# GpSimd's powers of two: multiply and add zero, where it multiplied alone

## The chip, the cores and the metric

The kernel runs on one core of one Trainium2 chip. The metric is the device time of one execution in microseconds (us). A core has TensorE (PE, with PEld for its weight loads), VectorE (DVE), ScalarE (ACT), GpSimd (POOL) and SyncE (SP), which each work through a queue of their own and wait for one another by semaphores.

## The reference

From one input x (1 x 2048 x 512, bf16) two branches are computed and mixed by a gate. Branch a is attention with 32 heads of 16; branch b mixes neighbouring rows and ends in an MLP of width 1792.

```
g = sigmoid((x * gate_w).sum(-1))
a:  q, k, v = x @ wqkv              # 32 heads of 16
    p = softmax(q k^T * 16 ** -0.5)
    a = (p v) @ wo
b:  h  = gelu(layernorm(x) @ w1);   quarters of h shifted by +1, -1, +2, -2 rows
    x1 = x + shifted(h) @ w2
    b  = x1 + gelu(layernorm(x1) @ w3) @ w4
out = g * a + (1 - g) * b
```

## The kernel before

**Units.** The rows are 4 chunks of 512 queries. A unit is one chunk and four heads: 32 units. In a unit the scores of one head against 128 keys are a block of 128 x 512 (keys by queries), 64 blocks a unit. TensorE writes blocks into PSUM (`score`, line 749); the exponentials turn them into bf16 weights; TensorE multiplies those with v and a column of ones into an accumulator (`attend_block`, line 924), so that the sum of the weights comes along; `finish_unit` divides.

**Slots.** Blocks go through slots. A slot has three blocks for ScalarE, which takes their exponential in one instruction (`expo`, line 912, 128 x 1536). The scores carry a factor of 65536/ln 2, which the exponential's scale takes out again. From slot 34 on a slot can hold two blocks for ScalarE (128 x 1024) and a third, in the PSUM tile `dsc`, whose exponential VectorE and GpSimd work out without ScalarE. `wants_whole` chooses these; there are 254 of them, taken in 127 pairs.

**An exponential without ScalarE** (`whole`). The score is 65536 times the exponent of two.

- `dump` (VectorE, line 845) adds a bias, clamps and converts to int32 in a tile `y`, of which there are two buffers, shared with the output's `dd` (line 535). The high 16 bits of an element are the whole part of the exponent, the low 16 the fraction.
- `factor` (GpSimd, line 852) reads the low halves and makes a linear factor in f16, in the tile `once`, by a multiply and an add.
- `two` (GpSimd, line 858) reads the high halves, multiplies by 128 and writes 16-bit integers, whose bits are a bf16 power of two, in the tile `power`. Behind it the y buffer is free.
- When both blocks of a pair are there, VectorE makes three products over 128 x 1024: `square` (line 866, from `once` alone), `linear` (line 870, `power` times `once`) and `cubic` (line 883). `power`, `cube` and `once` are the three terms that TensorE sums in the accumulator in place of one exponential (`attend`).

There are three sets of (`power`, `once`, `cube`); two have these names, the third is cut out of a tile named `more`. At most two pairs are under way (`CHAINS`), and a new dump is planned only if a y buffer is free by the plan (`YBUFS` = 2).

**Order.** The instruction order on every engine is fixed when the kernel is built: a planner keeps a clock for each engine, and always issues what can start first by its own list of costs. For both GpSimd steps this cost is `POOLT` = 0.62 us, whatever their form; the clocks also keep VectorE's instructions that share the port with GpSimd apart from GpSimd's. On the chip the engines then follow that order and wait where the plan was off. Between the attention blocks the planner puts the work of branch b (projections at line 217, `gelu_pair` at lines 357 to 390, layer norms with the transposed copies at line 347), and `fill` (line 1103) puts matmuls with a zero weight where TensorE would be idle.

Of the kernel before, what the change touches and what calls it, by code (L numbers as in the profile page):

```python
# [11 lines left out]
ALU = mybir.AluOpType  # L12
# [6 lines left out]
U16 = mybir.dt.uint16  # L19
# [12 lines left out]
def kernel(  # L32
# [13 lines left out]
    nc = tc.nc  # L46
# [101 lines left out]
    for j in range(4):  # L148
        src = A_wo.rearrange("(G j a d) n -> j a d G n", j=4, a=2, d=DH)[j]
        for a in range(2):  # L150
            nc.sync.dma_start(
                out=wo_pad[32 * j + 1:32 * j + 1 + DH, :, :].rearrange("d (G a) n -> a d G n", a=2)[a],
# [39 lines left out]
    def post(engine, rank, cost, fn, ready=0.0, shared=False):  # L192

        state["n"] += 1
        queue[engine].append((rank, state["n"], cost, fn, ready, shared or engine == "pool"))
# [626 lines left out]
    def whole(k, dsc, n, kt, j, ready):  # L822

        if whole_pair["open"] is None:
            whole_pair["chains"] += 1
            whole_pair["open"] = (n, j)
            whole_pair["tiles"] = (room.popleft(), [])
            r = 0  # L830
        else:
            whole_pair["open"] = None
            r = 1
            heads = {j, whole_pair["tiles"][1][0][1]}

            whole_pair["heads"] = () if whole_pair["heads"] and whole_pair["heads"][0] == n else (n, heads)
        whole_pair["last"] = k
        whole_pair["y"] += 1
        (power, once, cube), pair = whole_pair["tiles"]
        pair.append((kt, j))  # L840
        times = {}

        def dump(end):
            y = ypool.tile([P, CH], I32, tag="y", name="y")
            nc.vector.tensor_scalar(out=y[:], in0=dsc[:], scalar1=(127.0 + SHIFT) * 65536.0, scalar2=65536.0,  # L845
                                    op0=ALU.add, op1=ALU.max)
            dumped[k] = end
            halves = y[:].bitcast(U16).rearrange("p (n k) -> p n k", k=2)
            lo, hi = halves[:, :, 0], halves[:, :, 1]

            def factor(end):
                nc.gpsimd.tensor_scalar(out=once[:, r, :].bitcast(F16), in0=lo, scalar1=UK * LN2 / 65536.0, scalar2=UK * (UX - LN2 / 2),  # L852
                                        op0=ALU.mult, op1=ALU.add)
                if r == 1:
                    post("vector", 2, 0.68, square, end, True)

            def two(end):
                nc.gpsimd.tensor_scalar(out=power[:, r, :].bitcast(U16), in0=hi, scalar1=128.0, scalar2=None, op0=ALU.mult)  # L858
                times["power"] = end
                whole_pair["y"] -= 1  # L860

            post("pool", 1, POOLT, factor, end + 0.05)
            post("pool", 1, POOLT, two, end + 0.05)

        def square(end):
            nc.vector.tensor_tensor(out=cube[:].bitcast(F16), in0=once[:].bitcast(F16), in1=once[:].bitcast(F16), op=ALU.mult)  # L866
            post("vector", 2, 0.68, linear, lambda: max(end, times["power"]) if "power" in times else None, True)

        def linear(end):
            nc.vector.tensor_tensor(out=once[:], in0=power[:], in1=once[:].bitcast(F16), op=ALU.mult)  # L870
            both = state["credit"] > TWO and not state["done"]
            if both:
                post("vector", 2, 0.41, more, end, True)
            else:
                post("vector", 2, 0.68, cubic, end, True)

        def more(end):
            nc.vector.tensor_scalar(out=cube[:].bitcast(F16), in0=cube[:].bitcast(F16), scalar1=1.0, scalar2=None, op0=ALU.add)
            post("vector", 2, 0.68, lambda end: cubic(end, 2), end, True)

        def cubic(end, count=3):

            nc.vector.tensor_tensor(out=cube[:], in0=once[:], in1=cube[:].bitcast(F16), op=ALU.mult)  # L883
            whole_pair["chains"] -= 1
            products.append((n, pair, (power, cube) if count == 2 else (power, cube, once), end, (power, once, cube)))

        post("vector", 0, 0.69, dump, ready)
# [317 lines left out]
```

## Time and profile before

| | before |
|---|---|
| median of three runs | 920.33 us (919.62 to 920.62) |
| profiled execution | 923.89 us |
| its span | 920.9 us |
| mean granted clock of TensorE | 0.973 |
| GpSimd: line 852, multiply and add | 174 + 80 instructions, 736 and 730 ns in the mean |
| GpSimd: line 858, multiply | 174 + 80 instructions, 1530 and 1555 ns in the mean |

The profile is of one execution. The span runs from its first to its last instruction; the difference to the execution's own time lies around it. A line such as `L858 POOL TENSOR_SCALAR power<-y 128x512 uint16<-128x512 uint16 x174 | 266.2, 1530 | 0.0` is a group of instructions: source line, engine, operation, output and input with shape and type, count, busy us in all, mean ns of one, and the idle time of that engine just before them with what ended it. Idle time of an engine that others do not wait for costs nothing. A group under a name from the program, `power` or `more`, may be the same line with another buffer.

### The profile page before, as it was taken

To read this page: it belongs to the slowest core of one execution; us is meant where nothing else is said; L and a number is where in the kernel's file an instruction comes from. 1 tells how busy PE (TensorE), PEld (TensorE's weight loads), DVE (VectorE), ACT (ScalarE), POOL (GpSimd) and SP (SyncE) were. 2 spreads that over 40 slices of the span, in tenths; PEclk is the share of its full clock that TensorE was granted. 3 is DMA by queue.
4 is the path that set the end of the run, shared out by engine and by line. 5 is a ranking of instruction groups with operands and counts; after the bars stand their busy time and mean duration, and the time that the engine had idled before them with its cause. 6 is when DMAs were issued, how large, how long until landed. Compare 5 with 4: busy or idle time off the path is not lost.

```text
span 920.9 us, 15816 instructions
## 1 busy us (share of the span) xinstructions
PE 822.1 (89%) x5977; PEld 246.2 (27%) x5977; DVE 782.2 (85%) x1213; ACT 862.1 (94%) x735; POOL 580.4 (63%) x552
## 2 busy tenths in 40 slices
PE   8998988989898998998988899998899898899886
PEld 3222322222222222222222222222222222222221
DVE  5648699899999999888999887899876989998865
ACT  6899999999999999999999899999899999999984
POOL 3117576567686556887654887586566747698850
PEclk9999799999999999999999799999899999999988
DMA  9300100000002000001000000100000000000000
GB/s 232 100 14 13 59 2 12 13 13 14 9 7 92 13 13 13 13 4 34 13 13 13 1 13 14 36 13 13 2 12 14 13 31 1 18 13 14 14 13 23
DMA packets 30772, 22.22 MB, mean 24 GB/s; under 512 B 17256, under 2 KB 26216, under 8 KB 30696
## 3 DMA queue, kind: packets, MB, share of 16 engines
q1 hardware_dynamic: 29064, 20.04, 7.4%
q10 hardware_dynamic: 1632, 1.18, 0.5%
q8 instruction: 46, 0.75, 0.4%
q14 instruction: 30, 0.25, 0.1%
HBM read 17.04 MB, written 2.35 MB: 21 GB/s over the span
## 4 chain that ended last, share of the span: by engine, by line
DVE 38%; POOL 23%; PE 15%; issue 12%; ACT 9%; DMA 1%; POOLq 0%; DVEq 0%; ACTq 0%; SPq 0%
POOL power L858 9%; ACT pt L912 9%; POOL once L852 8%; DVE y L845 7%; PE stage L749 4%; PE acc L924 4%; DVE cube L866 4%; DVE once L870 4%; POOL more L858 4%; DVE cube L883 3%; POOL more L852 3%; DVE yh L390 2%; DVE more L866 2%; PE ps_y L217 2%; PE ps L217 2%
## 5 line engine op out<-in xcount | busy, mean ns | idle before, releaser
L912 ACT ACTIVATE pt<-stage 128x1536 bf16<-128x1536 f32 (+1 forms) x694 | 830.9, 1307 | 41.3 <-PE stage L749 17.8
L749 PE MATMUL stage<-qT,kT 32*128 32x512 bf16 x1794 | 277.6, 391 | 45.0 <-ACT pt L912 26.0
L852 POOL TENSOR_SCALAR once<-y 128x512 f16<-128x512 uint16 x174 | 128.0, 736 | 220.3 <-DVE y L845 213.6
L858 POOL TENSOR_SCALAR power<-y 128x512 uint16<-128x512 uint16 x174 | 266.2, 1530 | 0.0
L845 DVE TENSOR_SCALAR y<-dsc 128x512 int32<-128x512 f32 x254 | 173.1, 683 | 54.2 <-PE dsc L749 23.9
L924 PE MATMUL acc<-pt,vp 128*17 128x512 bf16 (+1 forms) x1794 | 188.8, 393 | 8.7 <-DVE accsb L987 8.5
L749 PEld LDWEIGHTS <-kT 32*128 32x128 bf16 x2048 | 78.4, 91 | 297.8 <-issue 227.5
L858 POOL TENSOR_SCALAR more<-y 128x512 uint16<-128x512 uint16 x80 | 124.4, 1555 | 0.0
L924 PEld LDWEIGHTS <-vp 128*17 128x17 bf16 (+1 forms) x2302 | 67.2, 89 | 142.7 <-issue 124.3
L749 PE MATMUL dsc<-qT,kT 32*128 32x512 bf16 x254 | 98.5, 388 | 0.3 <-DVE y L845 0.3
L852 POOL TENSOR_SCALAR more<-y 128x512 f16<-128x512 uint16 x80 | 58.4, 730 | 59.4 <-DVE y L845 48.3
L217 PE MATMUL ps_y<-xnT,w 128*128 128x512 bf16 x288 | 84.6, 382 | 11.8 <-DVE yh L390 9.9
L866 DVE TENSOR_TENSOR cube<-once 128x1024 f16<-128x1024 f16 x87 | 79.2, 910 | 13.0 <-POOL once L852 12.7
L1103 PE MATMUL acc<-wq,zero 128*128 128x512 bf16 x254 | 89.4, 395 | 0.0
L870 DVE TENSOR_TENSOR once<-power,once 128x1024 bf16<-128x1024 bf16 x87 | 68.2, 784 | 1.6 <-POOL power L858 1.5
L217 PE MATMUL ps<-w,g2T 128*128 128x512 bf16 x224 | 67.9, 390 | 1.4 <-DVE x_sb L462 0.9
L883 DVE TENSOR_TENSOR cube<-once,cube 128x1024 bf16<-128x1024 bf16 x87 | 64.9, 745 | 1.1
L390 DVE TENSOR_SCALAR yh<-ps_y 128x512 bf16<-128x512 f32 x72 | 49.0, 681 | 2.2 <-PE ps_y L217 2.1
L866 DVE TENSOR_TENSOR more<-more 128x1024 f16<-128x1024 f16 x40 | 37.1, 927 | 5.6 <-POOL more L852 5.6
L370 ACT ACTIVATE sq<-sq 128x1024 bf16<-128x1024 bf16 x36 | 39.6, 1106 | 0.0
L924 PE MATMUL acc<-cube,vp 128*17 128x512 bf16 x174 | 33.3, 402 | 3.2 <-DVE cube L883 3.0
L217 PEld LDWEIGHTS <-w 128*128 128x128 bf16 x288 | 23.1, 97 | 45.7 <-issue 36.0
(101 smaller groups left out, 743.9 us busy)
## 6 DMA issues: line engine op xcount, KB each, us to landing
bcs<-rec_d SPq DMA_DIRECT2D x31, 256.0 KB
w<-in_B_w_dram SPq DMA_DIRECT2D x2, 1792.0 KB
x_sb<-in_A_x_dram SPq DMA_DIRECT2D x14, 128.0 KB
out_dram<-ot SPq DMA_DIRECT2D x14, 128.0 KB
w<-in_B_w_dram SPq DMA_DIRECT2D x2, 512.0 KB
wkv<-in_A_wqkv_dram ACTq DMA_DIRECT2D x1, 512.0 KB
wo_pad<-in_A_wo_dram SPq DMA_DIRECT2D x8, 64.0 KB
den<-accsb SPq DMA_DIRECT2D x31, 8.0 KB
```

The costliest lines, as they stand in the source:

```text
L217: nc.tensor.matmul(*args, **kwargs)
L390: nc.vector.tensor_scalar(out=yh[:, r, :], in0=ps[:], scalar1=0.5, scalar2=None, op0=ALU.mult)
L749: nc.tensor.matmul(out, lhsT=kT[G][32 * j:32 * j + 32, cc, o:o + P], rhs=qTs[(c, G)][32 * j:32 * j + 32, a, :], start=True, stop=True, til ...
L845: nc.vector.tensor_scalar(out=y[:], in0=dsc[:], scalar1=(127.0 + SHIFT) * 65536.0, scalar2=65536.0, op0=ALU.add, op1=ALU.max)
L852: nc.gpsimd.tensor_scalar(out=once[:, r, :].bitcast(F16), in0=lo, scalar1=UK * LN2 / 65536.0, scalar2=UK * (UX - LN2 / 2), op0=ALU.mult, o ...
L858: nc.gpsimd.tensor_scalar(out=power[:, r, :].bitcast(U16), in0=hi, scalar1=128.0, scalar2=None, op0=ALU.mult)
L866: nc.vector.tensor_tensor(out=cube[:].bitcast(F16), in0=once[:].bitcast(F16), in1=once[:].bitcast(F16), op=ALU.mult)
L870: nc.vector.tensor_tensor(out=once[:], in0=power[:], in1=once[:].bitcast(F16), op=ALU.mult)
L883: nc.vector.tensor_tensor(out=cube[:], in0=once[:], in1=cube[:].bitcast(F16), op=ALU.mult)
L912: nc.scalar.activation(out=pt[:, 0:w], in_=stages.pop(k)[:, 0:w], func=ACT.Exp, scale=LN2 / 65536.0)
L924: nc.tensor.matmul(accs[n][32 * j:32 * j + M, :], lhsT=lhsT, rhs=p, start=(kt == 0), stop=(kt == NT - 1), skip_group_check=True, tile_posi ...
L1103: nc.tensor.matmul(acc[:], lhsT=zero[:], rhs=wq[:, 0, :], start=False, stop=False, skip_group_check=True)
```

## The change

In `two`, the instruction on GpSimd gets a second step: after the multiplication by 128 it adds 0.0. Its input, its output and its place in the queue stay, and so do the planner's costs. All else is as before.

```diff
             def two(end):
-                nc.gpsimd.tensor_scalar(out=power[:, r, :].bitcast(U16), in0=hi, scalar1=128.0, scalar2=None, op0=ALU.mult)
+                nc.gpsimd.tensor_scalar(out=power[:, r, :].bitcast(U16), in0=hi, scalar1=128.0, scalar2=0.0, op0=ALU.mult, op1=ALU.add)
                 times["power"] = end
                 whole_pair["y"] -= 1
```

## The prediction

> **What bounds the kernel now.** I read the first part of the page (busy time by engine), then the chain that ended last, then the costliest groups, and then went to the waits of single lines. "power" and "more" are both names of the tile that the changed line 858 writes; "more" is the third set of buffers.
>
> ```profile
> PE 822.1 (89%) x5977; PEld 246.2 (27%) x5977; DVE 782.2 (85%) x1213; ACT 862.1 (94%) x735; POOL 580.4 (63%) x552
> ...
> DVE 38%; POOL 23%; PE 15%; issue 12%; ACT 9%; DMA 1%; POOLq 0%; DVEq 0%; ACTq 0%; SPq 0%
> POOL power L858 9%; ACT pt L912 9%; POOL once L852 8%; DVE y L845 7%; PE stage L749 4%; PE acc L924 4%; DVE cube L866 4%; DVE once L870 4%; POOL more L858 4%; DVE cube L883 3%; POOL more L852 3%; DVE yh L390 2%; DVE more L866 2%; PE ps_y L217 2%; PE ps L217 2%
> ...
> L852 POOL TENSOR_SCALAR once<-y 128x512 f16<-128x512 uint16 x174 | 128.0, 736 | 220.3 <-DVE y L845 213.6
> L858 POOL TENSOR_SCALAR power<-y 128x512 uint16<-128x512 uint16 x174 | 266.2, 1530 | 0.0
> L845 DVE TENSOR_SCALAR y<-dsc 128x512 int32<-128x512 f32 x254 | 173.1, 683 | 54.2 <-PE dsc L749 23.9
> ...
> L858 POOL TENSOR_SCALAR more<-y 128x512 uint16<-128x512 uint16 x80 | 124.4, 1555 | 0.0
> ...
> L390 DVE TENSOR_SCALAR yh<-ps_y 128x512 bf16<-128x512 f32 x72 | 49.0, 681 | 2.2 <-PE ps_y L217 2.1
> ```
>
> ScalarE, 94% busy with the exponentials, is the floor. GpSimd is busy only 63%, yet it holds 23% of the chain, and line 858 alone 13% (9 and 4), about 120 us. Both facts go together if GpSimd's work comes in bursts: idle in total, late inside a burst. So the question is not how much GpSimd time is saved but how much idle time of ScalarE goes back to GpSimd. ScalarE's idle time is seen by stretches of the span:
>
> ```profile
> 0.00:23.00 23.00, 20.15 (x107) 7.54 (x107) 12.73 (x30) 15.77 (x19) 8.93 (x30) 1.00 0.95 232
> 23.00:46.00 23.00, 22.12 (x123) 6.45 (x122) 15.98 (x38) 18.55 (x20) 3.22 (x3) 1.00 0.36 100
> ...
> 897.00:920.00 23.00, 14.79 (x90) 4.35 (x87) 13.29 (x17) 11.72 (x9) 0.00 (x0) 0.89 0.07 23
> sum 920.00, PE 822.06 PEld 246.25 DVE 782.15 ACT 862.07 POOL 580.37; mean PE 20.55 PEld 6.16 DVE 19.55 ACT 21.55 POOL 14.51
> ```
>
> The columns are PE, PEld, DVE, ACT, POOL busy, the granted clock, the DMA share and GB/s. Without the first two stretches and the last, ScalarE is busy 862.07 - 15.77 - 18.55 - 11.72 = 816.0 of 851 us: 35 us of idle time in the middle. That is the most that any change to this pipeline can give.
>
> **The change part by part.** One operand pair changes in one instruction, which is issued 254 times (174 + 80). Nothing is moved, no wait is added, the planner's cost for it (0.62) stays, so every queue keeps its order. The output is the same number. What can change is the duration of line 858.
>
> ```profile
> L858 POOL TENSOR_SCALAR power<-y x174: 1479/1485/2449, 66.2 to 890.7; 128x512 uint16<-128x512 uint16 x174
> ...
>   DVE y L845: 24.2, 43
>   DVE dd L535: 7.5, 8
>   DVE once L870: 1.5, 4
>   DVE more L870: 0.9, 3
> ```
>
> ```profile
> L852 POOL TENSOR_SCALAR once<-y x174: 610/618/1643, 65.7 to 890.1; 128x512 f16<-128x512 uint16 x174
> ```
>
> (Minimum, median and maximum in ns, the first and last start, and for line 858 who waited for it: us and times.) Line 852 is the nearest row there is: the same engine, the same tile y (its other 16-bit halves, same stride), the same 512 elements a partition, but multiply and add; median 618 ns. Line 858 multiplies alone and takes 1485 ns. So the form with more arithmetic takes 867 ns less. Two differences remain between them: the missing second step, and the output type (uint16 against f16). If the missing step is the cause, the changed line takes 618; if the type is, it stays at 1485. For the type, the nearest rows are on VectorE: line 845 converts f32 to int32 at 683 ns, line 390 f32 to bf16 at 681 ns, so there an integer output costs nothing. It is another engine, hence only a leaning. I take 618 ns, with 1485 as the other end for a change without effect; an end above 1485 is priced among the rivals.
>
> The Trainium skill has a rule that speaks against this change: "GPSIMD Engine Reference", section 3.1 on side-by-side cycle accounting, says that an elementwise body of at most two operations is bound by the port at about 1.03 cycles an element. By it one step and two cost the same, 512 elements some 440 ns, and the change would do nothing. Line 852 fits it (618 ns with what an instruction costs besides); line 858 at 1485 ns doesn't, so this trace shows that something in line 858's form falls outside it.
>
> GpSimd's busy time would drop by 254 x 0.867 = 220 us, to 360. Nearly all of that lies beside other work. What reaches the end is seen in one burst, in order of time:
>
> ```profile
> 168.52 1.49 POOL L858 TENSOR_SCALAR power<-y 128x512 uint16<-128x512 uint16 x1
> ...
> 170.04 0.69 DVE L845 TENSOR_SCALAR y<-dsc 128x512 int32<-128x512 f32 x1 [1.00 <-POOL power L858]
> ...
> 170.65 0.41 DVE L347 COPY xnT<-ps_t 128x512 bf16<-128x512 bf16 x1
> ...
> 171.12 1.02 PE L217 MATMUL ps_y<-xnT,w 128*128 128x512 bf16 x4 [0.99 <-DVE xnT L347]
> ...
> 172.56 1.02 ACT L912 ACTIVATE pt<-stage 128x1024 bf16<-128x1024 f32 x1 [0.58 <-PE dsc L749]
> ```
>
> There are two y buffers, and line 858 reads a buffer last. The third dump of a burst (line 845) waits 1.00 us for it; behind the dump in VectorE's queue stands the copy of xnT, for which TensorE waits 0.99; behind that stand the next scores, for which ScalarE waits 0.58. At 618 ns line 858 would have ended at 169.14, before the dump was due, and the three waits go. GpSimd's pace in the burst falls from 0.62 + 1.49 = 2.1 us a dump to 1.24, near the one exponential of 1.02 that passes with each dump.
>
> How much of it there is in all: line 858 held VectorE up 58 times for 34.1 us (24.2 + 7.5 + 1.5 + 0.9), 0.59 us each, less than the 0.867 saved, so nearly all of these waits go. The squares wait too, for the first step of GpSimd queued behind line 858:
>
> ```profile
> DVE cube L866 <- POOL once L852: 12.7, 21, 1.2
> ...
> DVE more L866 <- POOL more L852: 5.6, 11, 1.0
> ```
>
> All VectorE waits for GpSimd in the timeline come to 55 us (95 waits). To see what arrives at ScalarE I went through its gaps in the timeline between 64 and 897 us: 71 gaps of 0.15 us or more, 31.1 us. In 31 of them, 13.9 us, VectorE waited for GpSimd within the 4 us before (at 5 us it would be 16.8). The first and the last of the 31:
>
> ```profile
> 85.19 10.49 ACT L912 ACTIVATE pt<-stage 128x1536 bf16<-128x1536 f32 x9 [0.70 <-PE stage L749]
> ...
> 883.53 2.79 ACT L912 ACTIVATE pt<-stage 128x1536 bf16<-128x1536 f32 x2 [0.47 <-PE stage L749]
> ```
>
> So 55 us of VectorE waits become about 14 us of ScalarE gaps, a quarter; the rest is slack. I take 13 us: nearly all of the 13.9, a little kept back because a few squares will still wait for line 852. What is late next is TensorE: the remaining 17 us of gaps stay, in which VectorE itself waited for TensorE's scores. The sum: the profiled execution took 923.89 us (its span 920.9), so 923.89 - 13 = 910.9; it lies 3.6 us above the median of the runs, 920.33, against which the forecast is 907.3, in round terms 907. Its own range: half of the attributed gaps, 7 us (913.5), to three quarters of all 31 us, 23 us (897), since a pipeline that stays near its plan may also lose gaps that I couldn't trace.
>
> **The rivals.** *No effect*: the type of the output, not the missing step, costs the time, or the single step was never slow for the reason I think. Line 858 stays at about 1485 ns, GpSimd at 580 us, the time at 920.3. For it: no row shows a uint16 output on GpSimd with two steps. Against: the 683 and 681 ns on VectorE. The rule of the page named above would give this time too, though it would have the present line fast already.
>
> *A wait takes its place*: line 858 gets fast, but VectorE loses as much where the two meet.
>
> ```profile
> L866 DVE TENSOR_TENSOR cube<-once x87: 623/1059/1092, 68.4 to 890.8; 128x1024 f16<-128x1024 f16 x87
> ```
>
> The square mostly starts together with line 858 and then takes 1059 ns where the fastest took 623. If GpSimd's earlier starts cost the second and third product of each of the 127 pairs (87 + 40) 0.4 us too, VectorE has up to 127 x 0.8 = 102 us more work; a quarter of it would reach ScalarE, 25 us; half of that cancels the gain: 920. Against: GpSimd starts as many instructions as before, and each would be over sooner.
>
> *Slower*: the slow path is the type's, and there the added step costs on top. It is priced by the nearest rows of GpSimd:
>
> ```profile
> L478 POOL MEMSET hT<- 128x8 bf16 x1 | 0.1, 100 | 0.0
> ```
>
> An instruction with next to no data takes 100 ns. Two steps in line 852 cost 618 - 100 = 518, one 260; in line 858 one step costs at most 1485 - 100 = 1385. With 260 more, the 58 waits grow by 15 us and a burst gets longer; by a quarter to a half, 4 to 8 us: 924 to 928. With 1385 more, line 858 takes 2870 ns and the pair with 736 beside it 3.6 us; the dumps come on average each (890.7 - 66.2) / 253 = 3.26 us, so GpSimd would set the pace from about 2500 ns on, and 254 x 3.6 = 914 us between the start at 66 and a tail of 29 gives 1009. I name 928 as its time, the near row being the one of the same engine and the same arithmetic.
>
> **How the numbers follow.** Line 858 near 618 ns with the waits gone: 0.66, 897 to 913.5, at 907. No effect: 0.18, at 920.3. The place taken: 0.05, at 920. Slower: 0.11, at 924 and more. I give the first so much since two rows that differ in so little differ by 867 ns in the direction of the change, and no more than that since one of their two differences isn't touched. A run of this kernel repeats within about 0.1%, and a change of 0.2% (1.8 us) is about what can be told from none. So faster 0.66, same 0.23, slower 0.11. The range runs from 896 to 922: it takes in the forecast's own range and the two cases of no change, and leaves out the slower case and a twentieth below, together under two tenths.
>
> **What would show it.** Right: line 858's median near 618 ns; GpSimd near 360 us; VectorE's waits for line 858 from 34 us to under 5; ScalarE's middle idle time from 35 to about 22 us; line 858 gone from the top of the chain. Line 858 still at 1485 puts the type in the step's place and the time at 920. Line 858 at 618 with ScalarE's idle time unchanged makes my attribution of gaps wrong: the gaps would then be TensorE's own, with the GpSimd waits merely nearby. The prediction would also fail if line 852 or the products of lines 866 to 883 got slower by as much.

## The result, and the profile after

The changed kernel takes 881.03 us (880.12 to 891.32, 4 runs) against 919.98 us (918.77 to 920.62, 4 runs): ratio 0.9604, 95% interval 0.9532 to 0.9675. It is 39 us faster; the forecast was 13, and 881 lies below the range of 896 to 922. The profiled execution took 881.57 us, its span is 879.5.

From the page of the kernel after, the engines' busy time, the chain, and the groups that answer to those of before:

```profile
PE 790.0 (90%) x5875; PEld 253.0 (29%) x5977; DVE 779.6 (89%) x1213; ACT 849.6 (97%) x735; POOL 403.6 (46%) x552
...
ACT 51%; issue 20%; PE 20%; DVE 8%; POOL 1%; DMA 1%; ACTq 0%; DVEq 0%; POOLq 0%
...
L912 ACT ACTIVATE pt<-stage 128x1536 bf16<-128x1536 f32 (+1 forms) x694 | 823.6, 1402 | 11.7 <-PE stage L749 4.8
...
L852 POOL TENSOR_SCALAR once<-y 128x512 f16<-128x512 uint16 x174 | 144.2, 829 | 306.3 <-DVE y L845 297.7
L845 DVE TENSOR_SCALAR y<-dsc 128x512 int32<-128x512 f32 x254 | 173.5, 684 | 33.6 <-PE dsc L749 29.1
...
L858 POOL TENSOR_SCALAR power<-y 128x512 uint16<-128x512 uint16 x174 | 127.8, 734 | 0.0
```

GpSimd has gone from 23% of the chain to 1%, ScalarE from 9% to 51%: the kernel is now bound by its exponentials. Line 858 by itself (minimum, median, maximum in ns), and who still waits for it (us, times):

```profile
L858 POOL TENSOR_SCALAR power<-y x174: 611/617/1581, 66.2 to 848.0; 128x512 uint16<-128x512 uint16 x174
...
  DVE dd L535: 1.0, 3
  DVE y L845: 0.9, 3
```

The median is 617 ns where 618 was taken; VectorE's waits for this line fell from 34.1 to 1.9 us. Where the span went is seen in the stretch without the first 46 and the last 24 us, the same work in both kernels (the columns are those of the busy times above, in us, then the clock, the DMA share and GB/s; the first row is the kernel before, the second the kernel after):

```profile
46.00:897.00 851.00, 764.99 (x5661) 227.91 (x5661) 740.15 (x1130) 816.03 (x690) 568.22 (x519) 0.97 0.05 17
```

```profile
46.00:855.60 809.60, 735.43 (x5567) 235.88 (x5665) 737.56 (x1130) 804.18 (x690) 391.49 (x519) 0.99 0.06 17
```

The stretch is 41.4 us shorter, all of what the span lost. ScalarE's idle time in it fell from 35.0 to 5.4, which is 29.6; and its busy time, with the same 690 instructions, from 816.0 to 804.2, which is 11.8. The forecast counted 13 of the first and nothing of the second.

### The profile page after: what moved, and what is told of

Read it like the earlier page. It is cut to its first block, busy times and chain, and to the rows that moved or that the text cites. A ratio compares the mean times of both kernels' runs of the same rounds, so it can differ in the third digit from the quotient of the medians.

```text
span 879.5 us, 15714 instructions
## 1 busy us (share of the span) xinstructions
PE 790.0 (90%) x5875; PEld 253.0 (29%) x5977; DVE 779.6 (89%) x1213; ACT 849.6 (97%) x735; POOL 403.6 (46%) x552
## 4 chain that ended last, share of the span: by engine, by line
ACT 51%; issue 20%; PE 20%; DVE 8%; POOL 1%; DMA 1%; ACTq 0%; DVEq 0%; POOLq 0%
ACT pt L912 48%; PE stage L749 6%; PE acc L924 5%; ACT sq L370 3%; PE ps L217 2%; PE ps_y L217 2%; DVE y L845 1%; DVE st L305 1%; DVE cube L866 1%; PE ps_o L217 1%; PE ps_v L217 1%; DMA wkv<-in_A_wqkv_dram 1%; DVE once L870 1%; DVE cube L883 1%; PE ps_q L217 1%
## 5 line engine op out<-in xcount | busy, mean ns | idle before, releaser
L912 ACT ACTIVATE pt<-stage 128x1536 bf16<-128x1536 f32 (+1 forms) x694 | 823.6, 1402 | 11.7 <-PE stage L749 4.8
L852 POOL TENSOR_SCALAR once<-y 128x512 f16<-128x512 uint16 x174 | 144.2, 829 | 306.3 <-DVE y L845 297.7
L845 DVE TENSOR_SCALAR y<-dsc 128x512 int32<-128x512 f32 x254 | 173.5, 684 | 33.6 <-PE dsc L749 29.1
L749 PEld LDWEIGHTS <-kT 32*128 32x128 bf16 x2048 | 89.7, 91 | 287.8 <-issue 241.2
L858 POOL TENSOR_SCALAR power<-y 128x512 uint16<-128x512 uint16 x174 | 127.8, 734 | 0.0
L1103 PE MATMUL acc<-wq,zero 128*128 128x512 bf16 x219 | 75.7, 386 | 1.7 <-issue 1.7
L883 DVE TENSOR_TENSOR cube<-once,cube 128x1024 bf16<-128x1024 bf16 x87 | 71.4, 820 | 1.1
L866 DVE TENSOR_TENSOR cube<-once 128x1024 f16<-128x1024 f16 x87 | 70.6, 811 | 1.5 <-POOL once L852 1.5
L858 POOL TENSOR_SCALAR more<-y 128x512 uint16<-128x512 uint16 x80 | 61.0, 763 | 0.0
L374 DVE SCALAR_TENSOR_TENSOR g2T<-sq,yh 128x1024 bf16<-128x1024 bf16 x28 | 36.4, 1298 | 0.3 <-ACT sq L370 0.3
L883 DVE TENSOR_TENSOR more<-more 128x1024 bf16<-128x1024 bf16 x40 | 32.3, 807 | 0.4
## 6 DMA issues: line engine op xcount, KB each, us to landing
x_sb<-in_A_x_dram SPq DMA_DIRECT2D x14, 128.0 KB
out_dram<-ot SPq DMA_DIRECT2D x14, 128.0 KB
```

The costliest lines, as they stand in the source:

```text
L749: nc.tensor.matmul(out, lhsT=kT[G][32 * j:32 * j + 32, cc, o:o + P], rhs=qTs[(c, G)][32 * j:32 * j + 32, a, :], start=True, stop=True, til ...
L912: nc.scalar.activation(out=pt[:, 0:w], in_=stages.pop(k)[:, 0:w], func=ACT.Exp, scale=LN2 / 65536.0)
L1103: nc.tensor.matmul(acc[:], lhsT=zero[:], rhs=wq[:, 0, :], start=False, stop=False, skip_group_check=True)
```

## The experiments

**The forms by themselves.** With nothing else on GpSimd, nine forms on 128x512 tiles, two tiles in turn: for instance `ts(out=d, in0=hi, scalar1=128.0, scalar2=None, op0=ALU.mult)` for `mul_u` and `op0=ALU.add, op1=ALU.mult` for `addmul_u`.

> This kernel leaves the whole computation out: it copies x to the output and, with nothing else on GpSimd or VectorE, runs nine forms of the elementwise instruction, six of each, on 128x512 tiles, so only the durations on GpSimd count. Theory 'single step' (an instruction with one arithmetic step goes a slow way whatever its types): multiply alone is near 1485 ns with a uint16 output, with f16 and with dense bf16 in and out; every two-step form is near 617 ns, mult-mult and add-mult too. Rival 'one pair' (only multiply-then-add has a fast way): mult-mult and add-mult are near 1485 ns or above, like the single steps. Rival 'integer' (the slow way needs an integer output and a single step): multiply alone into f16 and bf16 is near 617 ns, into uint16 near 1485. Add alone tells whether the slow way belongs to the multiply or to any single step.

The groups on GpSimd, by form (busy us and mean ns of one):

```profile
L62 POOL TENSOR_SCALAR add_u<-src 128x512 uint16<-128x512 uint16 x6 | 9.0, 1492 | 0.0
L63 POOL TENSOR_SCALAR mul_bf<-bsrc 128x512 bf16<-128x512 bf16 x6 | 9.0, 1492 | 0.0
L56 POOL TENSOR_SCALAR mul_u<-src 128x512 uint16<-128x512 uint16 x6 | 8.9, 1488 | 1.0 <-DVE src L40 1.0
L58 POOL TENSOR_SCALAR mul_f<-src 128x512 f16<-128x512 uint16 x6 | 8.9, 1487 | 0.0
L57 POOL TENSOR_SCALAR muladd_u<-src 128x512 uint16<-128x512 uint16 x6 | 3.7, 618 | 0.0
L59 POOL TENSOR_SCALAR muladd_f<-src 128x512 f16<-128x512 uint16 x6 | 3.7, 618 | 0.0
L60 POOL TENSOR_SCALAR mulmul_u<-src 128x512 uint16<-128x512 uint16 x6 | 3.7, 618 | 0.0
L61 POOL TENSOR_SCALAR addmul_u<-src 128x512 uint16<-128x512 uint16 x6 | 3.7, 617 | 0.0
L64 POOL TENSOR_SCALAR muladd_bf<-bsrc 128x512 bf16<-128x512 bf16 x6 | 3.7, 617 | 0.4
```

All four single-step forms take 1487 to 1492 ns, all five two-step forms 617 to 618, in all types and steps tried. "Single step" holds; "one pair" and "integer" fall. The Trainium skill, "GPSIMD Engine Reference", section 3.1 on side-by-side cycle accounting, has a rule for at most two operations that would make one step and two cost the same; these rows lie some 870 ns apart, and the measurement decides.

**Another second step.**

```diff
-... scalar1=128.0, scalar2=0.0, op0=ALU.mult, op1=ALU.add)
+... scalar1=128.0, scalar2=1.0, op0=ALU.mult, op1=ALU.mult)
```

> The changed kernel with a second multiply by 1.0 in place of the added zero; the result is the same number. 'Single step': line 858 at 617 ns, time at the changed kernel's 881. 'One pair': line 858 at 1485 ns or above, time at 920 or above.

Measured: 879.29 us (878.13 to 883.26), ratio 0.9558 (0.9503 to 0.9613), line 858 at a median of 617 ns. The added zero is nothing special: a multiply by 1.0 does the same in the kernel, and an add before the multiply did in the forms.

**The slow form in the other instruction.**

```diff
-... in0=lo, scalar1=UK * LN2 / 65536.0, scalar2=UK * (UX - LN2 / 2), op0=ALU.mult, op1=ALU.add)
+... in0=lo, scalar1=UK * LN2 / 65536.0, scalar2=None, op0=ALU.mult)
```

> The changed kernel, in which line 852 leaves out its added constant and multiplies alone (so the linear factor lacks its constant and the output is another). Line 858 stays at two steps. 'Single step': line 852 goes to about 1485 ns, line 858 stays at 617, and GpSimd has the same work per dump as before the change. If the time is set by GpSimd's pace in bursts, whichever of its two instructions is slow, it comes back to 920 or somewhat above (squares wait for line 852, so 920 to 930). If only the lateness of the y buffers behind line 858 mattered, it gives back less: 885 to 905. 'Integer': line 852 stays at 617 and the time at 881.

Measured: 1009.8 us (1009.25 to 1012.85), ratio 1.0975 (1.0914 to 1.1035). Both expected times are missed, by 80 us and more. The duration came as "single step" says. From the rows of lines 852 and 866 in this kernel:

```profile
L852 POOL TENSOR_SCALAR once<-y x174: 1482/1522/2450, 66.3 to 976.5; 128x512 f16<-128x512 uint16 x174
...
  DVE cube L866: 65.2, 68
  DVE more L866: 30.1, 30
```

GpSimd does about the same work as before the change (613 against 580 us busy), but the squares, VectorE's next step, need line 852's result and wait 95 us for it, where they waited 18. Line 858 is fast here, yet VectorE still waits 31 us for it, nearly as long as before: it stands in the queue behind the slow line 852. (Its granted clock is lower too, 0.938; by the spread between runs told below, some 5 us for each 0.01, that would be about a quarter of the 90 us above the kernel before, an estimate.) A slow instruction costs by its place: behind line 852 there is a waiting VectorE at once, behind line 858 there are the square and a second buffer first. GpSimd's total says little about the time.

**Half of the instructions slow: the first block of each pair.**

```diff
+                if r == 0:
+                    (multiply alone)
+                else:
+                    (multiply and add zero)
```

> The kernel before, with the two-step form of line 858 for the second block of every pair only: 127 of the 254 instructions stay at 1485 ns. Theory 'every gap': nearly all idle time of ScalarE's middle part came from GpSimd's bursts, in proportion to the GpSimd time lost: half of the 39 us is gained, 900. Theory 'burst': two y buffers take up one slow instruction but not several in a row, so half of them cost much less than half: 884 to 892, with ScalarE's middle idle time near 10 us. Theory of the prediction (only the 14 us of gaps close behind a GpSimd wait are GpSimd's): nothing follows for the size, since the full change gave three times as much.

Measured: 904.1 us (903.44 to 907.71), ratio 0.9833 (0.9767 to 0.9899); ScalarE's idle time in the middle stretch is 831.40 - 810.71 = 20.7 us:

```profile
46.00:877.40 831.40, 737.60 (x5566) 229.79 (x5663) 733.66 (x1130) 810.71 (x690) 476.54 (x519) 0.99 0.05 17
```

That is nearest to "every gap", on its slow side, and not "burst". But VectorE's waits for GpSimd hardly fell: 43 us in place of 55. Those that remain (line 859 is the multiply alone, line 869 the square; lines stand three lower here):

```profile
DVE y L845 <- POOL power L859: 14.2, 20, 1.3
DVE cube L869 <- POOL once L852: 13.0, 21, 1.5
...
DVE more L869 <- POOL more L852: 5.6, 11, 1.0
```

The squares wait as they did before the change, 18.6 us, though their own second block is fast: line 852 of the second block stands in GpSimd's queue behind the slow instruction of the first. Hence the mirror image:

**Half of the instructions slow: the second block.** As above with `r == 1`.

> The mirror of the half change: the first block of a pair gets the two-step form, the second keeps the multiply alone; again 127 of 254 instructions stay at 1485 ns, with the same GpSimd time as the half change (489 us busy, 904 us). Theory 'which wait': what costs is that the second block's line 852, and the third dump, wait behind the slow instruction of the first block; here neither does, so VectorE's waits for GpSimd fall from 43 us in the half change to under 12 and the time to 881 to 888. Theory 'GpSimd time': only the sum counts, 900 to 905. If the dumps of the following pair wait as much for the second block as they did for the first, it lies between, near 895.

Measured: 883.16 us (881.75 to 884.34), ratio 0.9616 (0.9567 to 0.9664). GpSimd's time is near that of the half before (503 against 489 us busy; the first row is from the page), ScalarE's middle stretch that of the full change:

```profile
PE 808.7 (92%) x5977; PEld 251.6 (29%) x5977; DVE 783.5 (89%) x1213; ACT 850.2 (97%) x735; POOL 503.0 (57%) x552
```

```profile
46.00:855.70 809.70, 751.67 (x5662) 233.37 (x5662) 741.46 (x1130) 804.15 (x690) 490.86 (x519) 0.99 0.06 17
```

VectorE's waits for GpSimd are 9.8 us, and the two rows that answer to the costly ones above have nearly gone:

```profile
DVE y L845 <- POOL power L859: 2.5, 8, 0.4
DVE cube L869 <- POOL once L852: 1.7, 4, 0.8
```

"Which wait" holds: with 127 slow instructions left, all but some 2 us of the gain is there (883.2 against 881.0, less than the runs of either kernel differ among themselves). It also answers a rival: that a slow GpSimd costs time because VectorE's own instructions take longer beside it. VectorE is busy 783.5 us here, 782.2 before the change and 779.6 after; it has no more work where the time is longer. What costs is the slow instruction that has other work of GpSimd queued behind it and VectorE waiting for that; the second block's has none that is urgent, and its 1.49 us pass beside the square.

**Slack for VectorE.** Lines 361 and 366 left out of both kernels.

> The kernel before with two of VectorE's instructions of each GELU left out (lines 361 and 366: 36 each, 18.8 and 25.9 us; the GELU is another function without them), order and everything else as it was. GpSimd keeps its slow line 858. Theory 'carried on': VectorE is so full that a delay GpSimd gives it travels on in its queue and reaches ScalarE long after, which my 4 us window missed; with slack in VectorE delays die out, so the kernel before gains 15 us or more (905 or less), and ScalarE's middle idle time falls from 35 us to under 22. Theory 'only near gaps': the far gaps have nothing to do with VectorE's queue, and leaving out work of a VectorE that is no floor gives under 8 us (over 911).

> The changed kernel with the same two instructions left out. ScalarE's middle idle time is already 5.4 us there, so 'carried on' says that there is little for VectorE's slack to give: 1 to 6 us, 875 to 880; and that the distance between the two kernels, 39 us with VectorE full, shrinks to 25 or less. 'Only near gaps': the distance stays 33 to 40.

Measured: the kernel before 910.38 us (907.02 to 911.93, 10 runs), ratio 0.9898 (0.9873 to 0.9924); the changed one 879.7 us (877.7 to 879.8, 4 runs). The gain of 9 us lies between the two theories' bounds (15 and 8), and so does the distance that is left, 31 us. The changed kernel lies 1 us under its 881.0, which was taken on another chip; that can't be told from no gain. ScalarE's idle time in the kernel before came down from 35.0 to 24.8 us (at a clock of 0.973 and 0.983). VectorE still waits 60 us for GpSimd, 5 more than before, so its slack takes up some of the delays; how far the rest are carried, this doesn't decide.

**A few slow instructions in the changed kernel.**

```diff
+                if r == 0 and n % 4 == 2:
+                    (multiply alone)
+                else:
+                    (multiply and add zero)
```

> The changed kernel with the multiply alone put back in the first block of a pair, in every fourth unit only (units 2, 6, 10 and so on; the first blocks carry the whole cost, as the two half changes showed). The changed kernel has hardly any gap of ScalarE between 64 us and the end, so nearly each gap here is made by these few slow instructions, and the time from VectorE's wait for GpSimd to ScalarE's gap can be read. 'Carried on': a good part of the gap time, a third or more, comes over 4 us after the last such wait, with VectorE busy without a break between; time 888 to 894, about a quarter of the 37 us. 'Only near gaps': over nine tenths of the gap time comes within 4 us of a wait, and the time is 884 to 887.

Measured: 889.46 us (887.01 to 895.86), ratio 0.9679 (0.9622 to 0.9735); the changed kernel on the same chip 879.05. 33 instructions are slow, and cost 10 us between the medians; but the two fastest runs (887.01 and 887.38, at a clock of 0.985) are only 8 us above its 879.05 at 0.987, so the time lies about the border of the two expectations and decides little. The places of the gaps say more. ScalarE has 18 gaps of 0.15 us or more between 64 and 866 us, 10.0 us in all. The order in every queue is that of the changed kernel, so the instructions of the two can be set side by side: six of the gaps, 2.5 us, stand in the changed kernel too, as large or larger. Of the other twelve, 7.5 us, three (2.6 us) come within 4 us of a VectorE wait for GpSimd of 0.15 us or more; nine (4.9 us) come later. One of the later ones, from the timeline of this kernel:

```profile
187.15 1.79 POOL L859 TENSOR_SCALAR power<-y 128x512 uint16<-128x512 uint16 x1
...
188.91 0.61 POOL L852 TENSOR_SCALAR once<-y 128x512 f16<-128x512 uint16 x1
...
189.56 1.09 DVE L869 TENSOR_TENSOR cube<-once 128x1024 f16<-128x1024 f16 x1 [1.08 <-POOL once L852]
190.57 1.21 DVE L374 SCALAR_TENSOR_TENSOR hT<-sq,yh 128x1024 bf16<-128x1024 bf16 x1
...
199.41 0.41 DVE L347 COPY xnT<-ps_t 128x512 bf16<-128x512 bf16 x1
...
199.87 0.59 PE L342 MATMUL ps_t<-ident,xn 128*128 128x128 bf16 x4 [0.58 <-DVE xnT L347]
...
201.64 1.45 ACT L915 ACTIVATE pt<-stage 128x1536 bf16<-128x1536 f32 x1 [0.80 <-PE stage L749]
```

The square waits 1.08 us at 189.56 for line 852, which waited behind the slow 1.79. From there VectorE has no idle time until after 201.64 (no row of it between carries one): it stays late because it has no slack to catch up with. At 199.41 its copy of xnT is late, TensorE waits 0.58, ScalarE 0.80 at 201.64: 12 us after the wait that began it. Two more slow instructions ran in the meantime without a wait of their own, and they added nothing: against the changed kernel, VectorE's instructions start already 4.2 us late just before this wait, 5.2 behind it, and 5.1 at 199.41. "Only near gaps" falls. "Carried on" holds for the time that a delay lives; its other sign, VectorE busy without a break in between, holds for two of the nine late gaps (1.0 us). In the other seven VectorE had idle time of its own on the way, nearly all of it waiting for TensorE, so a delay travels through several engines and not in VectorE's queue alone.

**A planner that knows.**

```diff
-            post("pool", 1, POOLT, two, end + 0.05)
+            post("pool", 1, 1.40, two, end + 0.05)
```

> The kernel before, with the multiply alone, but the planner is told 1.40 us for it in place of 0.62; the order is another one, and 50 blocks fewer (204 against 254) go past ScalarE. 50 more blocks cost ScalarE 50 x 0.43 = 21 us of the difference between its two widths, so its floor rises by that, from some 875 to some 896. If the 39 us were paid because the plan did not know of the slow instruction, the waits go and the time is 895 to 908, better than before's 919; if the slow instruction costs this much in any order, it stays at 915 or above.

Measured: 906.89 us (905.14 to 908.17), ratio 0.9873 (0.9823 to 0.9923). ScalarE's idle time in the middle stretch is 833.40 - 826.55 = 6.9 us:

```profile
46.00:879.40 833.40, 765.83 (x5644) 239.04 (x5642) 646.41 (x1006) 826.55 (x691) 474.32 (x419) 0.99 0.05 17
```

Most of ScalarE's idle time is gone, at the price of 10.5 us more of ScalarE's work than in the kernel before and 22 more than in the changed one. VectorE still waits 25 us for GpSimd, but with fewer blocks it is busy 76% in place of 85 and has slack. So an order that expects the slow instruction, with 50 blocks fewer, wins 12 of the 39 us.

**More blocks past ScalarE**, since it is the floor now: `CREDIT = 0.4` in place of 0.45, or `LATER = 0.35` in place of 0.4, each 260 blocks in place of 254.

> The changed kernel with the planner's CREDIT at 0.40 in place of 0.45, so that 260 blocks in place of 254 go past ScalarE. ScalarE is now busy for all but 5 us of the middle, and 6 blocks are 6 x 0.43 = 2.6 us of it. If ScalarE's pace is the floor, 1 to 3 us faster than the changed kernel; if VectorE, 89% busy, can't take 6 more blocks without delays, the same or slower.

> The changed kernel with the planner's LATER at 0.35 in place of 0.40: also 260 blocks past ScalarE, these in the last part of the span. If ScalarE's pace is the floor, 1 to 3 us faster than the changed kernel; if the end is set by the other work that is then left over for the last part, 1 to 4 us slower.

> The changed kernel as it is, on the same chip as the other three, for their comparison: 878 to 883.

Measured on one chip: 886.11 (882.18 to 889.05), 882.25 (880.85 to 883.33), and the changed kernel itself 879.05 us (877.88 to 891.30). Neither beats it: at about the same clock (0.987 to 0.988) they take 882.18 and 881.91 against its 879.05. In the first, ScalarE's busy time in the middle falls by 2.5 us (804.2 to 801.7), near the 2.6 that were expected, but its idle time rises from 5.4 to 8.7. In the second neither moves by more than 0.4 us there; why it is not faster stays open.

## Why the prediction was wrong, by its steps

- *Line 858 goes from 1485 to 618 ns*: right, 617, and the missing step is the cause; the forms show it without the rest of the kernel. The rivals "no effect" and "slower" fall with it.
- *GpSimd's busy time falls to 360 us*: 403.6. Two things were left out. Line 858's mean stays above its median (734 against 617 ns), so it gave back 202 us in place of 220; and line 852 grew by 22 us (736 to 829 ns in the mean). Beside one of VectorE's two-input instructions line 852 takes 839 ns in the mean before and 898 after, without one 620 and 626; it met one in 132 of its 254 runs before and in 182 after. "A wait takes its place" pointed the wrong way: the squares, which stood 1059 ns in the median beside the slow line 858, take 682 now; the products of line 883 grew from 745 to 820 in the mean.
- *Nearly all of VectorE's waits for line 858 go*: right, 34.1 to 1.9 us. (In the burst that was shown, the dump was due at 170.04 - 1.00 = 169.04, so an end at 169.14 is 0.1 us behind it and not before it; this changes nothing in the sum.)
- *13.9 us of ScalarE's gaps are GpSimd's, the other 17 us TensorE's own*: wrong, and the larger of the two errors. Of 35.0 us in the middle stretch 29.6 went. The step that failed is the window: a gap counted only if VectorE had waited for GpSimd within the 4 us before, and the rest of the 55 us of waits was called slack. A delay lives longer; the few slow instructions put 4.9 of 7.5 us of new gaps outside that window, one of them 12 us behind. The count with 8 us instead of 4 gives 25.6 of the 31 us in the timeline of before, with 10 us 29.1. Such a count proves nothing by itself, since 8 us before a random moment also hold such a wait 6 times in 10; the run with few slow instructions is what decides.
- *35 us is the most that any change to this pipeline can give*: wrong; 41.4 came in the profiled pair, and 39 at the same clock (below). This is the second error: the sum put the change of ScalarE's busy time at nothing, and it gave 11.8. That busy time is not a floor. Its row before, beside the one after shown above:

```profile
L912 ACT ACTIVATE pt<-stage 128x1536 bf16<-128x1536 f32 (+1 forms) x694 | 830.9, 1307 | 41.3 <-PE stage L749 17.8
```

Before, 694 x 1307 ns are 907 us of instructions in 831 busy us; after, 694 x 1402 ns are 973 us in 824. Instructions overlap, and the more so the better ScalarE is fed. How far is seen where it is never starved, in the kernel after (three narrow windows one after the other, so that the first column has the starts of single instructions of 1536 columns and the rows overlap):

```profile
289.43 2.95 ACT L912 ACTIVATE pt<-stage 128x1536 bf16<-128x1536 f32 x2
...
290.76 2.96 ACT L912 ACTIVATE pt<-stage 128x1536 bf16<-128x1536 f32 x2
...
292.09 3.47 ACT L912 ACTIVATE pt<-stage 128x1536 bf16<-128x1536 f32 x3
```

One starts each 1.33 us, though each lasts about 1.6 (2.95 - 1.33); behind a gap an instruction alone takes 1.45 (the row at 201.64 above). So an instruction that comes late loses a part of its overlap as well, and this part counts as busy. The sizes agree: in the middle stretch ScalarE has 123 gaps of any length before and 25 after; before, an instruction of 1536 columns that ends in a gap holds the engine for 1458 ns, one that is followed at once for 1330 (medians). The 98 gaps that went, at 0.13 us each, make 12.5 us, an estimate, near the 11.8. Across the kernels the two go together (the time is a median of runs; the rest, with the clock, is from the one profiled execution):

| kernel | time, us | VectorE's waits for GpSimd | ScalarE idle, middle | ScalarE busy, middle | clock |
|---|---|---|---|---|---|
| slow form in line 852 | 1009.8 | 126 | 111.5 | 826.4 | 0.938 |
| before | 920.0 | 55 | 35.0 | 816.0 | 0.973 |
| first block slow | 904.1 | 43 | 20.7 | 810.7 | 0.983 |
| second block slow | 883.2 | 10 | 5.6 | 804.2 | 0.987 |
| after | 881.0 | 4 | 5.4 | 804.2 | 0.984 |

From 35 us of idle time to 5, each us of it that goes takes about 0.4 us of busy time along (11.8 / 29.6). The Trainium skill, "Perfetto Trace Analysis", section "Identifying the Most-Contended Engine", takes occupancy for a fair measure of ScalarE's distance from its limit; here it left out 12 of 41 us (816.0 to 804.2, the same 690 instructions).

- *The profiled pair*: a part of its 41.4 us goes with the clock (0.973 before, 0.984 after). The 13 runs of the kernel before beside the second half change go from 913.67 us at 0.993 to 923.12 at 0.975, some 5 us for each 0.01. By that, about 6 us of the profiled pair go with the clock, an estimate. At about the same clock the distance is the same as between the medians: 919.05 at 0.985 (a run of before there) against 880.12 at 0.985. Whether the waits lower the clock, or the clock lengthens the waits, no run here separates.

## What to carry to other kernels

An elementwise instruction with one scalar step on GpSimd is worth a look: here a second step that does nothing made it 2.4 times as fast. Judge a late engine not by its total or by the gaps next to its waits, but by what stands behind each instruction in its queue and by how full the engine is that takes the delay on; if that one is nearly full, follow a delay until it meets slack. And take the ceiling of a gain from an engine's spacing of starts where it is well fed, not from its busy time.

## What the runs showed that was not expected

- Single-step and two-step forms differ by 870 ns at 128x512 in all types tried (1487 to 1492 against 617 to 618).
- The same slow duration costs 39 us in line 858, and 129 in line 852 (1009.8 against 881.0), with nearly the same GpSimd time (580 and 613 us) but a lower clock there; and in line 858 of the second block alone some 2.
- The spread between runs of one kernel goes with the granted clock: 913.67 us at 0.993, 923.12 at 0.975.
- GpSimd's multiply and add takes 620 ns without a two-input instruction of VectorE beside it, and 839 to 898 ns in the mean with one.
